# The first load of K in two parts, two small loads moved behind an activation, and w2 in four transfers

## The chip, the cores and the metric

The kernel runs on one core of a Trainium2 chip. The metric is the device time of one execution in microseconds; a time given for a kernel is the median of several executions. A profile comes from one further execution. Its span reaches from the first to the last instruction of the program; the execution's own time is a little longer.

## What is computed

A decoder step for a single token: an adaptive layer norm, attention with 32 query heads over a cache of 8 heads with 32768 positions each, and a small feed-forward layer. Cut to what matters:

```python
mod = (_silu(c) @ w_mod).reshape(c.shape[0], 6, 1, -1)      # c: 512, w_mod: 512 x 3072
sa, ca, ga, sb, cb, gb = (mod[:, i] for i in range(6))
h = _layernorm(x) * (1 + ca) + sa                            # x: one row of 512
q = h @ wq                                                   # 512 x 4096: 32 heads of 128
scores = einsum('bhqd,bhkd->bhqk', q, k) * 128 ** -0.5       # k_cache, v_cache: 8 x 32768 x 128
o = einsum('bhqk,bhkd->bhqd', softmax(scores), v)
x = x + ga * (o @ wo)                                        # wo: 4096 x 512
h = _layernorm(x) * (1 + cb) + sb
x = x + gb * (relu(h @ w1) @ w2)                             # w1: 512 x 1792, w2: 1792 x 512
```

All tensors are bf16. The two caches are 64 MB each, the weights some 15 MB together. All of it is read once, so that the kernel is above all one long stream of loads.

## The kernel before, in words

**The stream of loads.** `load` (L112) issues one load, and `stream_dma` (L154) issues its transfers on SyncE's queue (SP). The list `stream` (L163 to L169) fixes the order once: the first half of K of head 0, w_mod, wq, the second half of K of head 0, then K of the next head and V of this one in turn, for the last heads in halves, and at the end wo in four pieces (`WOP`, L47), w1 in one and w2 in five (`W2P`, L52: pieces of 5, 5, 2, 1 and 1 of the 14 tiles of 512 columns; a tile is 128 KB). `need` (L172) issues the loads of the list up to the one that is asked for.

A whole head of K or V is 8 MB: 128 partitions with 64 KB each, so that partition p holds 256 neighbouring positions of the cache. Half a head is 128 rows of 32 KB. The tiles of the stream come from a pool with three buffers of 64 KB per partition (`ring`, L81). The first of them takes w_mod and wq, the next K of head 0, the third K of head 1; V of head 0 waits until w_mod and wq have been used, and so on around the ring. Each transfer tells of its landing by one of eight semaphores, taken in turn, and a transfer waits until the one eight before it has landed.

The second half of K of head 0 (`UNEVEN`, L57 and L137 to L142) is split: all 128 rows without their last 512 bytes, then these last 512 bytes of 111 rows, then those of the other 17 rows. Behind the issue of V of head 0 stand 14 drains on SP (L145 to L147).

**The start.** `need(("wm",))` (L180) issues the first half of K and w_mod. c and x, one row of 512 each, are loaded by two small transfers on ScalarE's queue (ACT) into eight partitions each (L182 and L183); they are the first thing that ACT does. GpSimd meanwhile makes the identity matrices and constants, `eps_t` among them (L192), and VectorE (DVE) makes masks. When c and x have come, DVE (L248) and four matmuls (L254) turn them into columns (`xc`, L259). From these come silu(c) (`siluT`, L313 to L318, with an exponential on ACT) and the statistics of the layer norm (L282 to L306, with a square root on ACT, for which ACT loads another table of functions). DVE then turns the first half of K (L332). TensorE (PE) multiplies siluT with w_mod (L324) when w_mod has landed, and after the modulation has been brought into columns the first layer norm is applied and multiplied with wq (L396). The query heads are written into a block-diagonal form (`qbd`, L415).

**The heads.** For each head DVE transposes K in place (L441), PE computes the scores (L460), softmax follows (L473 to L509), and PE multiplies with V (L523, for most heads in a hardware loop). PE's and DVE's order is written out by hand (L637 to L735).

**The end.** After V of the last head come the projection with wo (L599 and L605), the second layer norm (L282 to L307), w1 (L765), relu (L776) and w2: for each piece of `W2P`, PE waits for its load and makes four matmuls for each of its tiles (L781 to L791). DVE multiplies by the gate (L793), adds x (L795), and SP stores the row (L796).

Of the kernel before, what the change touches and what calls it, by code (L numbers as in the profile page):

```python
# [9 lines left out]
BF16 = mybir.dt.bfloat16  # L10
F32 = mybir.dt.float32
ACT = mybir.ActivationFunctionType
# [5 lines left out]
def kernel(  # L18
# [14 lines left out]
    nc = tc.nc  # L33
    P = 128
    _, _, D = A_x.shape
# [13 lines left out]
    LAST = Hkv - 1  # L49
    LOOPED = Hkv - 2  # L50
    HALVED = LOOPED - 1
    W2P = [(0, 5), (5, 10), (10, 12), (12, 13), (13, 14)]  # L52
    W1P = [(0, KT)]

    OUT0, OUT1 = 30, 34
# [2 lines left out]
    SPACE = 14  # L58
    assert Dh == 128 and REP == 4 and D == 512 and FT == W2P[-1][1] and NTILE == 4
    scale = float(Dh) ** -0.5  # L60
# [9 lines left out]
    def wo_v(i):  # L70
        g0, n = WOP[i]
        return A_wo[g0 * REP * Dh:(g0 + n) * REP * Dh, :].rearrange("(p r) d -> p r d", p=P)
# [9 lines left out]
    const = ctx.enter_context(tc.tile_pool(name="const", bufs=1))  # L82
# [16 lines left out]
    def room(name, at, shape):  # L99

        n = 2
        for d in shape[1:]:
            n *= d
        return piece(name, at, n)[0:shape[0]].bitcast(F32)

    def piece(name, at, n):

        if name not in pieces:
            pieces[name] = ring.tile([P, NTILE * TK * Dh], BF16, tag="slot", name=name)
        return pieces[name][:, at:at + n]  # L110

    def load(key):  # L112
        kind = key[0]
        if kind == "wm":
            t = piece("wmq_sb", 0, WM).rearrange("p (kt n) -> p kt n", kt=KT)
            src = wm_v
        elif kind == "wq":
            t = piece("wmq_sb", WM, WQ).rearrange("p (kt n) -> p kt n", kt=KT)
            src = wq_v
        elif kind in "kv":  # L120
            g, steps = key[1], key[2]
            src = (kv if kind == "k" else vv)[g, :, TK * steps[0]:TK * (steps[-1] + 1), :]
            name = f"Ksb{g}" if kind == "k" else f"Vsb{g}"
            t = piece(name, TK * Dh * steps[0], TK * Dh * len(steps)).rearrange("p (j d) -> p j d", d=Dh)
        elif kind == "wo":
            g0, n = WOP[key[1]]
            t = piece("tail_sb", g0 * REP * D, n * REP * D).rearrange("p (r d) -> p r d", d=D)
            src = wo_v(key[1])
        elif kind == "w1":
            k0, k1 = W1P[key[1]]  # L130
            t = piece("tail_sb", WO + k0 * Dff, (k1 - k0) * Dff).rearrange("p (kt f) -> p kt f", f=Dff)
            src = w1_v[:, k0:k1]
        else:
            f0, f1 = W2P[key[1]]
            t = piece("tail_sb", WO + KT * Dff + f0 * D, (f1 - f0) * D).rearrange("p (f d) -> p f d", d=D)
            src = w2_v[:, f0:f1]
        if key == UNEVEN:  # L137
            row, src_row = (x.rearrange("p j d -> p (j d)") for x in (t, src))
            for rows, cols in (
                (slice(0, P), slice(0, EDGE)), (slice(0, MOST), slice(EDGE, None)), (slice(MOST, P), slice(EDGE, None)),  # L140
            ):
                stream_dma(row[rows, cols], src_row[rows, cols])  # L142
        else:
            stream_dma(t, src)
        if key[:2] == ("v", 0):  # L145
            for _ in range(SPACE):
                nc.sync.drain()  # L147
        if kind in "kv":
            for i, u in enumerate(steps):
                loaded[(kind, g, u)] = t[:, TK * i:TK * (i + 1), :]  # L150
        else:
            loaded[key] = t

    def stream_dma(dst, src):  # L154
        i = nc.sync.dma_start(out=dst, in_=src)  # L155
        tc.stamp_issue_order_token(i.ins, "sp_stream")
        if last_loop:

            tc.add_manual_dep(i.ins, last_loop[0], mybir.DependencyInfo(
                mybir.DependencyClass.NoSync, mybir.DependencyReason.DATA))  # L160

    whole, halves = [(0, 1, 2, 3)], [(0, 1), (2, 3)]
    stream = [("k", 0, halves[0]), ("wm",), ("wq",), ("k", 0, halves[1])]  # L163
# [4 lines left out]
    stream += [("v", LAST, (0, 1)), ("v", LAST, (2,)), ("v", LAST, (3,))] + [("wo", i) for i in range(len(WOP))]  # L168
    stream += [("w1", i) for i in range(len(W1P))] + [("w2", i) for i in range(len(W2P))]  # L169
    pos = [0]  # L170

    def need(key):  # L172
        while key not in loaded:
            load(stream[pos[0]])
            pos[0] += 1
        return loaded[key]
# [1 line left out]

    piece("wmq_sb", 0, WM + WQ)
    wm_sb = need(("wm",))  # L180
    cx_row = const.tile([16, D // 8], BF16)
    for i, row in enumerate((c[0], A_x[0, 0])):  # L182
        nc.scalar.dma_start(out=cx_row[8 * i:8 * i + 8], in_=row.rearrange("(a n) -> a n", a=8))  # L183

    ident_bf = const.tile([P, P], BF16)
    make_identity(nc, ident_bf[:])
    ident_f = const.tile([P, P], F32)
# [2 lines left out]
    nc.gpsimd.memset(ones_f[:], 1.0)  # L190
    eps_t = const.tile([P, 1], F32)
    nc.gpsimd.memset(eps_t[:], eps)  # L192
    R0 = WM + WQ
    sel = piece("wmq_sb", R0 + 2048, 4 * P).rearrange("p (x c) -> p x c", x=4)
    ib = ident_bf[:]
    nc.vector.tensor_copy(
        out=sel.rearrange("p (h par) (a c) -> p h par a c", h=2, a=4),
        in_=AP(ib.tensor, ib.offset, [ib.ap[0], [64, 2], [1, 2], [0, 4], [2, 32]]),
# [8 lines left out]
        out=mask16.rearrange("p (s q) -> p s q", q=REP),  # L207
        in_=AP(ident_f[:].tensor, ident_f[:].offset, [ident_f[:].ap[0], [0, 4], [1, REP], [REP, P // REP]]),
# [4 lines left out]
    for n in sorted({n * REP for _, n in WOP}):  # L213
        cmask[n] = const.tile([P, P // n], F32, name=f"cmask{n}")
        nc.vector.tensor_reduce(
            out=cmask[n][:], in_=ident_f[:].rearrange("p (c r) -> p c r", r=n), op=ALU.add, axis=AX.X,
# [3 lines left out]
            out=rsel_f[:], in_=ident_f[:].rearrange("p (c r) -> p r c", r=n), op=ALU.add, axis=AX.X,  # L220
# [6 lines left out]
        out=smask[:], in_=ident_f[0:16, 0:16].rearrange("p (s q) -> p s q", q=REP), op=ALU.add, axis=AX.X,  # L227
# [7 lines left out]
        out=place32[:], in_=ident_f[:].rearrange("p (j m) -> p m j", m=32), op=ALU.add, axis=AX.X,  # L235
# [4 lines left out]
        out=rowpick[:, OUT0:OUT1], in_=ident_f[:].rearrange("p (j m) -> p j m", m=32), op=ALU.add, axis=AX.X,  # L240
# [5 lines left out]
    nc.vector.tensor_copy(out=cx_sel[:], in_=cmask[8][0:16, 0:2])  # L246
    cx_bd = piece("wmq_sb", R0 + 2048 + 4 * P, D)[0:16].rearrange("p (b n) -> p b n", b=8)
    nc.vector.tensor_tensor(  # L248
        out=cx_bd, in0=cx_row[:].unsqueeze(1).to_broadcast([16, 8, D // 8]),
# [70 lines left out]
    def to_rows(dst, src_T, w, n):  # L320

        for kt in range(KT):
            for j in range(n):
                nc.tensor.matmul(  # L324
                    dst[j // 4][32 * (j % 4):32 * (j % 4) + 1, :], lhsT=src_T[:, kt:kt + 1],
                    rhs=w[:, kt, j * 512:(j + 1) * 512], start=(kt == 0), stop=(kt == KT - 1),
                    skip_group_check=True,
                )

    for u in range(2):  # L330
        t = need(("k", 0, u)).rearrange("p j d -> p (j d)").bitcast(F32)
# [5 lines left out]
    to_rows(mod_ps, siluT, wm_sb, 6)  # L337
    mod_rows = room("wmq_sb", R0, [P, 2, 512]).rearrange("p (i n) -> p i n", i=2)
    nc.scalar.copy(out=mod_rows[:, 0, :], in_=mod_ps[0])
# [22 lines left out]
    def four_rows(e, name):  # L362

        r_ps = (end_b[0][:, 1, :] if end_b else bank(f"{name}_ps"))[0:OUT1, 0:P]
        nc.tensor.matmul(
            r_ps, lhsT=rowpick[:], rhs=e.rearrange("p m kt -> p (m kt)"), start=True, stop=True,
        )
        return r_ps

    gb_rows = const.tile([OUT1, P], F32)  # L370
    gb_exp = room("wmq_sb", R0 + 2048 + 8 * P, [P, 32, KT]).rearrange("p (m kt) -> p m kt", kt=KT)
    nc.scalar.copy(out=gb_rows[:], in_=four_rows(expand(modT_sb[:, 5 * KT:6 * KT], gb_exp), "gb"))
# [6 lines left out]
        out=nca[:], in0=modT_sb[:, KT:2 * KT], scalar1=-1.0, scalar2=-1.0, op0=ALU.mult, op1=ALU.add,  # L379
# [3 lines left out]
        out=ncb[:], in0=modT_sb[:, 4 * KT:5 * KT], scalar1=-1.0, scalar2=-1.0, op0=ALU.mult, op1=ALU.add,  # L383
# [9 lines left out]
    for kt in range(KT):  # L393
        for i in range(2):
            for a in range(4):
# [3 lines left out]
                )  # L399
    q_cols = room("wmq_sb", R0, [P, 2, 512]).rearrange("p (i n) -> p i n", i=2)  # L400
    qT_sb = const.tile([P, Hq], BF16)
    for i in range(2):
        nc.vector.transpose(out=q_cols[:, i, :], in_=q_ps[i])
        nc.scalar.copy(
            out=qT_sb[:, 16 * i:16 * (i + 1)], in_=q_cols[:, i, :].rearrange("p (h r) -> p h r", r=32)[:, :, 0],
# [231 lines left out]
    with tc.manual_schedule(engines={mybir.EngineType.PE, mybir.EngineType.DVE}):  # L637
# [54 lines left out]
        for u in (2, 3):  # L692
# [49 lines left out]
            out=x1T[:], in0=x1T[:], scalar=1.0, in1=xT, op0=ALU.mult, op1=ALU.add, accum_out=stat2[:, 0:1],  # L742
# [31 lines left out]
        for f0, f1 in ((0, FT // 2), (FT // 2, FT)):  # L774
            nc.vector.transpose(out=hidT[:, f0:f1], in_=hid_v[:, f0:f1])
            nc.scalar.activation(  # L776
                out=AP(hb.tensor, hb.offset + 32 * f0 + 31, [hb.ap[0], [32, f1 - f0]]),
                in_=hidT[:, f0:f1, 0], func=ACT.Relu,
            )

        for part, (f0, f1) in enumerate(W2P):  # L781
            w2_sb = need(("w2", part))
            for ft in range(f0, f1):
                for i in (0, 2, 1, 3):
                    row = OUT0 + i
# [41 lines left out]
```

## Time and profile before

| | |
|---|---|
| time, median of 3 runs | 354.11 us (354.06 to 354.18) |
| profiled execution, its own time | 354.42 us |
| its span | 352.6 us |
| busy: PE, DVE, ACT, POOL | 77%, 55%, 5%, 2% of the span |
| bytes moved by DMA | 149.57 MB, mean 424 GB/s |
| transfers of the stream from issue to landing, median | 33.8 us |

How to read the views: the page gives, for each engine, the share of the span in which it was busy, and for the DMA queues the packets, the megabytes and the time that the packets took as a share of sixteen DMA engines. The view by windows gives the same for stretches of the span: length, busy time of PE, of its weight loads (PEld), DVE, ACT and POOL with the number of instructions in brackets, then the granted clock of PE, the share of the DMA engines and their rate. A packet is counted whole where it starts, so that a short stretch can show a share over 1. The DMA part of a stretch gives the packets, their megabytes and their share for each queue: q1 is SP's queue, q10 is ACT's. The chain of work that ended last is followed back from the last instruction: start, duration, what it was. The timeline has start, duration, engine, line, operation, tiles and, in brackets, how long the engine was idle before and what ended that.

### The profile page before, as it was taken

What the parts mean: (1) busy time and instruction counts of PE and PEld (TensorE: products, weight loads), DVE (VectorE), ACT (ScalarE), POOL (GpSimd) and SP (SyncE); (2) the same over time, 40 slices, a digit from 0 to 9 for tenths busy, and PEclk for the clock granted to TensorE, in tenths of its full rate; (3) what the DMA queues carried; (4) which work ended last, traced back from release to release, by engine and by line L of the source; (5) the groups of instructions that cost most, each with busy time, mean ns of one, the idle gap of its engine ahead of it and who ended that gap; (6) DMA issues with size and microseconds to landing.
All of it is one profiled execution on the core that took longest, in us unless ns stands there. A gap on an engine that the chain in (4) does not pass through costs nothing. (4 is left out here: it accounts for less than half of the span.)

```text
span 352.6 us, 3544 instructions
## 1 busy us (share of the span) xinstructions
PE 272.3 (77%) x1310; PEld 111.8 (32%) x1310; DVE 195.6 (55%) x167; ACT 18.7 (5%) x37; POOL 6.0 (2%) x26
## 2 busy tenths in 40 slices
PE   0054980695999679884988499976999999789994
PEld 0021330232333224331333233322444443234442
DVE  7662563983079513965099316956674293743142
ACT  1200003001000010001000100001000100011000
POOL 3000000000000000000000000000000000000000
PEclk9996895698999969998999979996999999999999
DMA  8999989999999999999999999999999999999995
GB/s 353 404 432 456 468 387 461 446 401 446 439 424 440 416 439 446 401 455 446 409 453 446 409 453 431 426 394 439 446 414 427 450 429 424 431 453 398 432 426 213
DMA packets 5222, 149.57 MB, mean 424 GB/s; under 512 B 604, under 2 KB 988, under 8 KB 1628
## 3 DMA queue, kind: packets, MB, share of 16 engines
q1 hardware_dynamic: 5180, 149.43, 98.5%
q8 instruction: 8, 0.13, 0.1%
q14 instruction: 2, 0.02, 0.0%
q10 hardware_dynamic: 32, 0.00, 0.0%
HBM read 149.42 MB, written 0.00 MB: 424 GB/s over the span
## 5 line engine op out<-in xcount | busy, mean ns | idle before, releaser
L441 DVE STREAM_TRANSPOSE Ksb<-Ksb 128x4096 f32<-128x4096 f32 (+1 forms) x34 | 131.5, 3912 | 57.6 <-DMA Ksb<-in_A_k_cache_dram 57.6
L460 PE MATMUL S_ps<-Ksb,qbd 128*128 128x512 bf16 x512 | 118.9, 385 | 19.2 <-DVE Ksb L441 18.3
L523 PE MATMUL o_ps<-Vsb,P_g 128*16 (+1 forms) x512 | 124.3, 401 | 10.9 <-ACT P_g L497 10.0
L460 PEld LDWEIGHTS <-qbd 128*128 128x128 bf16 x512 | 49.2, 97 | 84.9 <-issue 27.6
L523 PEld LDWEIGHTS o_ps<-Vsb,P_g 128*16 x320 | 30.4, 95 | 60.0 <-issue 31.8
L523 PEld LDWEIGHTS <-P_g 128*16 128x16 bf16 x192 | 16.7, 90 | 22.9 <-issue 0.4
L473 DVE TENSOR_REDUCE m_p<-S_ps 128x1 f32<-128x1024 f32 x7 | 8.6, 1223 | 21.8 <-PE S_ps L460 21.8
L502 DVE STREAM_TRANSPOSE P_g<-P_g 128x1024 bf16<-128x1024 bf16 x8 | 10.0, 1245 | 15.6 <-ACT P_g L497 15.6
L494 ACT ACTIVATE nbias<-Mb_ps 128x1 f32<-128x1 f32 x8 | 1.4, 171 | 269.5 <-PE Mb_ps L492 269.5
L324 PE MATMUL mod_ps<-wmq_sb,siluT 128*1 128x512 bf16 x24 | 3.6, 624 | 9.9 <-DMA wmq_sb<-in_w_mod_dram 9.9
L332 DVE STREAM_TRANSPOSE Ksb<-Ksb 128x4096 f32<-128x4096 f32 x2 | 8.8, 4424 | 1.7 <-DMA Ksb<-in_A_k_cache_dram 1.7
L478 PE MATMUL mT_ps<-ident_f,m_p 128*1 128x128 f32 x8 | 2.2, 270 | 8.9 <-DVE m_p L473 7.9
L497 ACT ACTIVATE P_g<-S_ps,nbias 128x1024 bf16<-128x1024 f32 x8 | 8.9, 1114 | 0.2
L560 PE MATMUL acc_ps<-mask_sb,Y 16*128 16x4 f32 x16 | 3.4, 282 | 5.1 <-DVE Y L556 5.1
L552 DVE SCALAR_TENSOR_TENSOR o_ps<-o_ps,Linv,smask 16x512 f32<-16x512 f32 x8 | 5.8, 720 | 2.8 <-PE o_ps L523 2.8
L254 PE MATMUL xc_ps<-cx_sel,wmq_sb 16*128 16x2 bf16 x4 | 0.3, 172 | 8.7 <-DVE wmq_sb L248 8.7
L590 DVE CAST o_sb<-o_ps 128x4 bf16<-128x4 f32 (+2 forms) x4 | 0.7, 167 | 11.1 <-PE o_ps L586 11.1
L415 POOL TENSOR_TENSOR qbd<-qrep_sb,rowpick 128x64 bf16<-128x64 bf16 x8 | 2.4, 299 | 228.0 <-PE S_ps L460 198.3
L509 DVE RECIPROCAL Linv<-L_ps 16x1 f32<-16x1 f32 x8 | 1.0, 126 | 8.3 <-PE L_ps L506 8.3
L556 DVE TENSOR_REDUCE Y<-o_ps 16x128 f32<-16x512 f32 x8 | 5.4, 679 | 0.3
L635 PE MATMUL spare_ps<-qbd,ident_bf 128*128 128x512 bf16 x18 | 5.4, 381 | 0.0
L396 PE MATMUL q_ps<-wmq_sb,hT 128*1 128x512 bf16 x32 | 3.6, 626 | 2.3 <-DMA wmq_sb<-in_A_wq_dram 2.3
(114 smaller groups left out, 71.6 us busy)
## 6 DMA issues: line engine op xcount, KB each, us to landing
Ksb<-in_A_k_cache_dram SPq DMA_DIRECT2D x5, 4096.0 KB, 22.9
Vsb<-in_A_v_cache_dram SPq DMA_DIRECT2D x5, 4096.0 KB, 36.5
wmq_sb<-in_A_wq_dram SPq DMA_DIRECT2D x1, 4096.0 KB, 28.1
Vsb<-in_A_v_cache_dram SPq DMA_DIRECT2D x2, 2048.0 KB, 41.1
Ksb<-in_A_k_cache_dram SPq DMA_DIRECT2D x1, 4032.0 KB, 37.2
wmq_sb<-in_w_mod_dram SPq DMA_DIRECT2D x1, 3072.0 KB, 18.9
tail_sb<-in_A_wo_dram SPq DMA_DIRECT2D x1, 2048.0 KB, 23.2
tail_sb<-in_B_w_dram SPq DMA_DIRECT2D x1, 1792.0 KB, 30.6
```

What stands on the lines that cost most here:

```text
L324: nc.tensor.matmul(dst[j // 4][32 * (j % 4):32 * (j % 4) + 1, :], lhsT=src_T[:, kt:kt + 1], rhs=w[:, kt, j * 512:(j + 1) * 512], start=(kt ...
L332: nc.vector.transpose(out=t, in_=t)
L396: nc.tensor.matmul(q_ps[i][32 * a:32 * a + 1, :].rearrange("o (h e) -> o h e", e=32), lhsT=hT[:, kt:kt + 1], rhs=wq_f[:, kt, i, a], start= ...
L441: t = nc.vector.transpose(out=KTt.bitcast(F32), in_=KTt.bitcast(F32))
L460: nc.tensor.matmul(S_ps_tiles[g], lhsT=qbd[g % 2][:, hp, 4 * (7 - s):4 * (7 - s) + P], rhs=KTv[:, 16 * sl:16 * sl + 16, h, :, par], start= ...
L473: behind_loop(nc.vector.reduce_max(out=m_p[:], in_=S_g.rearrange("p g f -> p (g f)"), axis=AX.X))
L497: nc.scalar.activation(out=P_g[:], in_=S_g.rearrange("p g f -> p (g f)"), func=ACT.Exp, bias=nbias[:], scale=scale, accum_out=l_g[:],)
L502: behind_loop(nc.vector.transpose(out=P_g[:], in_=P_g[:]))
L523: nc.tensor.matmul(o_tiles[g][:], lhsT=PT, rhs=Vx, start=first, stop=False, skip_group_check=True)
L552: nc.vector.scalar_tensor_tensor(out=o, in0=o, scalar=Linv_tiles.pop(g)[:], in1=smask[:].unsqueeze(2).to_broadcast([16, 4, Dh]), op0=ALU.m ...
L556: nc.vector.tensor_reduce(out=Y[:], in_=o.rearrange("p s d -> p d s"), op=ALU.add, axis=AX.X)
L635: nc.tensor.matmul(spare[0], lhsT=ident_bf[:], rhs=qbd[0][:, :, 0:P], start=True, stop=True)
```

## The change

Three edits. The first transfer of the stream, the first half of K of head 0, is issued as 16 rows and then the other 112. The transfers of c and x are written behind `eps_t`, and behind a new activation on one element of it; a dependency without a semaphore keeps them behind that activation in ACT's own order. And w2 comes in pieces of 6, 5, 2 and 1 tiles.

```diff
-    W2P = [(0, 5), (5, 10), (10, 12), (12, 13), (13, 14)]
+    W2P = [(0, 6), (6, 11), (11, 13), (13, 14)]
...
                 stream_dma(row[rows, cols], src_row[rows, cols])
+        elif key == stream[0]:
+            for rows in (slice(0, 16), slice(16, P)):
+                stream_dma(t[rows], src[rows])
         else:
             stream_dma(t, src)
...
     wm_sb = need(("wm",))
-    cx_row = const.tile([16, D // 8], BF16)
-    for i, row in enumerate((c[0], A_x[0, 0])):
-        nc.scalar.dma_start(out=cx_row[8 * i:8 * i + 8], in_=row.rearrange("(a n) -> a n", a=8))
-
     ident_bf = const.tile([P, P], BF16)
...
     nc.gpsimd.memset(eps_t[:], eps)
+    warm = const.tile([1, 1], F32)
+    first = nc.scalar.activation(out=warm[:], in_=eps_t[0:1], func=ACT.Exp)
+    cx_row = const.tile([16, D // 8], BF16)
+    for i, row in enumerate((c[0], A_x[0, 0])):
+        d = nc.scalar.dma_start(out=cx_row[8 * i:8 * i + 8], in_=row.rearrange("(a n) -> a n", a=8))
+        tc.add_manual_dep(d.ins, first.ins.name, mybir.DependencyInfo(
+            mybir.DependencyClass.NoSync, mybir.DependencyReason.DATA))
```

In the built program SP has as many transfers as before, one more at the front and one fewer at the end. ACT's first table load now stands ahead of c and x, with the new activation. The semaphores of the transfers move by one: the 17-row piece of K's second half now waits for the sixteen rows of the first half, K of head 1 for c. On DVE the reciprocal of the first layer norm (L306) stands ahead of the transposes of K (L332) instead of behind them.

## The prediction

> **What bounds the kernel now.** I read the page first (busy shares, DMA queues), then the chain of work that ended last in order of time, then stretches of DMA traffic.
>
> ```profile
> DMA  8999989999999999999999999999999999999995
> q1 hardware_dynamic: 5180, 149.43, 98.5%
> 338.50 11.12 DMA tail_sb<-in_B_w_dram
> 349.62 0.04 issue
> 349.66 0.29 PE end_ps L788 x4
> 349.95 0.02 issue
> 349.98 0.29 DVE o_rows L793
> 350.27 0.02 issue
> 350.30 0.28 DVE o_bf L795
> ```
>
> One queue, the one that SP issues to, carries 149.43 MB and keeps the sixteen DMA engines busy for 98.5% of the span. The two slices below 9 tenths that matter are the first and the last. The chain ends with the last weight transfer, landing at 349.62, and 1 us of small work behind it. Three stretches of 4.83 us, from the view by windows, show that nothing is lost in between:
>
> ```profile
> 43.43:48.26 4.83, 4.83 (x24) 2.12 (x23) 4.75 (x3) 0.00 (x0) 0.00 (x0) 1.00 1.01 436
> 60.00:64.83 4.83, 0.06 (x1) 0.16 (x2) 4.55 (x2) 0.00 (x0) 0.00 (x0) 0.50 1.00 434
> 79.00:83.83 4.83, 2.88 (x13) 1.07 (x11) 1.72 (x3) 0.00 (x0) 0.30 (x1) 1.00 1.00 434
> ```
>
> The last two columns are the DMA share (1.00) and the rate (434 GB/s), whatever PE and DVE do. So the time is: when the engines get their first bytes, plus what each has to move, plus the tail. Every engine works through its own list in order; a microsecond lost by one engine at the start is still missing at the end. That decides how the change is to be priced: only its first and last transfers, and anything that makes an engine stand still.
>
> **The rate of one engine, and the start.** The DMA part for a stretch in the middle (63.00 to 67.83 us), then the first transfers by windows of 0.2 us, then the DMA part for 1.7 to 2.7 us:
>
> ```profile
> q1 hardware_dynamic: 32, 2.10, 100.2%
> ```
> ```profile
> 1.50:1.70 0.20, 0.00 (x0) 0.00 (x0) 0.20 (x1) 0.03 (x1) 0.20 (x2) 1.00 0.02 3
> 1.70:1.90 0.20, 0.00 (x0) 0.00 (x0) 0.20 (x2) 0.20 (x1) 0.20 (x3) 1.00 2.95 821
> 1.90:2.10 0.20, 0.00 (x0) 0.00 (x0) 0.20 (x2) 0.20 (x1) 0.20 (x1) 1.00 3.54 984
> 2.10:2.30 0.20, 0.00 (x0) 0.00 (x0) 0.20 (x1) 0.20 (x1) 0.20 (x1) 1.00 1.42 492
> 2.30:2.50 0.20, 0.00 (x0) 0.00 (x0) 0.20 (x1) 0.20 (x1) 0.20 (x2) 1.00 0.45 164
> 2.50:2.70 0.20, 0.00 (x0) 0.00 (x0) 0.20 (x1) 0.20 (x1) 0.20 (x1) 1.00 0.44 164
> ```
> ```profile
> q1 hardware_dynamic: 16, 0.52, 175.6%
> ```
>
> In the middle, 32 packets of 64 KB take 1.002 x 16 x 4.828 / 32 = 2.42 us each: 27.1 GB/s for one engine, so a row of 32 KB takes 1.21 us. A packet is counted where it starts, and 164 GB/s in 0.2 us is one packet of 32 KB: 5, 6, 3, 1 and 1 engines begin in the five windows, on average at 2.04 us, the last one 0.8 us behind the first. These sixteen first packets take 1.756 x 16 x 1.0 / 16 = 1.76 us each, 0.55 us more than later ones.
>
> **Part 1, c and x behind an activation.** The timeline around them:
>
> ```profile
> 0.73 0.59 ACTq L183 DMA_DIRECT2D cx_row<-in_c_dram  x1
> 0.74 0.38 SPq L155 DMA_DIRECT2D Ksb<-in_A_k_cache_dram  x1
> 1.35 0.28 ACTq L183 DMA_DIRECT2D cx_row<-in_A_x_dram  x1
> 1.67 1.28 ACT L313 ACT_TABLE_LOAD   x1 [1.67 <-PEq L811]
> 1.73 0.10 POOL L192 MEMSET eps_t<- 128x1 f32 x1
> 2.12 20.71 SPq L155 DMA_DIRECT2D Ksb<-in_A_k_cache_dram  x4
> 7.99 0.68 DVE L248 TENSOR_TENSOR wmq_sb<-cx_row,pick 16x512 bf16<-16x512 bf16 x1 [1.50 <-DMA cx_row<-in_A_x_dram]
> 10.98 0.16 DVE L318 TENSOR_TENSOR siluT<-xc,sig 128x4 bf16<-128x4 f32 x1
> 12.85 8.77 DVE L332 STREAM_TRANSPOSE Ksb<-Ksb 128x4096 f32<-128x4096 f32 x2 [1.71 <-DMA Ksb<-in_A_k_cache_dram]
> 20.11 3.57 PE L324 MATMUL mod_ps<-wmq_sb,siluT 128*1 128x512 bf16 x24 [9.91 <-DMA wmq_sb<-in_w_mod_dram]
> ```
>
> The table load moves up to about 0.73 and ends near 2.0; eps_t is there at 1.83; the activation takes some 0.2 us; c is issued near 2.2 for 0.73, x near 2.8. They then queue behind more rows of K on each engine: x took 6.6 us from issue to the multiplication at 7.99, so it would come near 9.5, and up to 8 us later if those rows are slow. siluT (11.14) has 9 us until w_mod lands at 20.1, and w_mod moves with the same queue. Cost: nothing; uncovered it would be 1.5 us. What ACT does behind it (L313 on) waits for xc anyhow. The gain: c is generated at the same moment as K's first descriptors, and its issue takes 0.59 us where x takes 0.28. Up to 0.3 us earlier start for K, counted below.
>
> The extra transfer at the front shifts the eight DMA semaphores: the 17-row piece of K's second half now waits until the sixteen rows have landed, K of head 1 for c. Queued behind both on SP is the whole stream. But SP's first four K issues already end only at 22.83 (2.12 + 20.71), and the engines come to what is behind them after 38 us. Covered by 15 us.
>
> **Part 2, sixteen rows, then 112.** For it: every engine gets one descriptor at once. If all begin with the first window, 2.04 - 1.8 = 0.24 us, with c out of the way up to 0.3 more. I take 0.4.
>
> Against it: those sixteen rows go to sixteen neighbouring partitions, and the sixteen engines write there together. In a 128-row load each engine has eight partitions. The trace has one place where engines write into the partitions of others: the odd pieces of K's second half (111 and 17 rows of 512 B) near 39 us, while the other thirteen engines are already on K of head 1. The DMA parts for 38.60 to 38.98, 38.98 to 39.40 and 41.20 to 42.00 us:
>
> ```profile
> DMA packets 64, 0.87 MB, mean 2291 GB/s; under 512 B 15, under 2 KB 51, under 8 KB 51
> ## 3 DMA queue, kind: packets, MB, share of 16 engines
> q1 hardware_dynamic: 64, 0.87, 576.3%
> ```
> ```profile
> q1 hardware_dynamic: 54, 0.03, 21.7%
> ```
> ```profile
> q1 hardware_dynamic: 12, 0.79, 232.6%
> ```
>
> The middle one is short rows alone: 0.217 x 16 x 0.42 / 54 = 27 ns each. In the first, 13 packets are over 8 KB; 5.763 x 16 x 0.38 = 35.04 us, less 36 x 0.027 and about 0.14 for 15 completions, leaves 33.93, or 2.61 us each. The third has their second packets: 2.326 x 16 x 0.8 / 12 = 2.48. Against 2.42 each of the thirteen loses 0.19 + 0.06 = 0.25 us, and the 128 short rows are eight for each engine's eight partitions: 32 ns a row, where its bytes alone are 19 ns. I read this as a path into a group of partitions that has one engine's rate and is shared. It is an inference: a slower memory would look alike.
>
> If so, the sixteen rows take 16 x 1.21 / G us, with G such groups among sixteen partitions. Ends: G = 16, no sharing, 1.21; G = 2 (eight neighbours a group), 9.7. The trace does not show which eight partitions are a group. I take the middle step, G = 4: **4.84 us, 3.63 more** than now.
>
> [...]
>
> The 112 rows are seven for each engine, and runs of seven no longer lie on the groups of eight. Ends: none meets another, nothing; each meets another all the time, 7 x 1.21 = 8.5 us. I let the worst engine meet one other in three of its seven rows: **3.6 us**. The worst engine counts, since the end waits for the last.
>
> **Part 3, w2 in four.** The last piece (one tile, 128 KB) stays. Each engine has eight packets and one completion fewer; at the tail (DMA part for 349.0 to 349.3 us)
>
> ```profile
> q1 hardware_dynamic: 23, 0.02, 16.6%
> ```
>
> a packet takes 0.166 x 16 x 0.3 / 23 = 35 ns, most of it bytes. Ends: 0 and 9 x 0.02 = 0.2; I take 0.05 us gained. The piece before the last now feeds eight matmuls; four take 0.29 us at the end (chain), so at worst they push the last four back by 0.3, at best not at all. I take 0.
>
> **Sum.** 354.42 us is the profiled execution (span 352.6, 1.8 around it), 0.31 over the median of the three runs, 354.11. 354.42 + 3.63 + 3.64 - 0.4 - 0.05 = 361.2; against the median **360.9 us**.
>
> **Rivals.**
> - *No shared path* (other side). The thirteen engines lost their 0.25 us to something else, and sixteen engines may write to sixteen partitions at full rate. Then only the start counts: 0.1 us (stagger gone, first packets longer) to 0.9 (0.24 + 0.3 + part of the 0.55 + w2). I take 0.5: 353.6. It decides if all the sharing costs less than 0.5 us. For it: the 512 B rows themselves never took over 27 ns beside busy engines. Against it: the loss where they crossed. 0.30.
> - *The rows stay with their engines.* The sixteen rows are dealt to the engines that have these partitions in a 128-row load, so nothing crosses, but few engines start early, and the change does not do what it says: 354.0. 0.05.
> - *Row by row.* Of the 112 rows each engine takes every sixteenth, and all move together over sixteen neighbours: 8 x 4.84 = 38.7 us for 9.7, 29 more: 383. 0.04.
> - The forecast: 0.61, by itself from 357.5 (second term nothing) to 363 (both terms some way up).
>
> **Numbers.** About 0.2% (0.7 us) is what a measurement here tells from no change. Faster by more: 0.08, the better quarter of the first rival. Within: 0.22 of it and 0.05 of the second, 0.27. Slower: 0.61 + 0.04 = 0.65. Cases of both signs hold much of the chance, so the range goes from the first rival's middle to the top of the forecast: 353.5 to 363, which leaves out about 0.2.
>
> **What would show it.** The first transposes of K (at 12.85) would begin near 19.5 to 20, and the rate from 2 to 6 us would be near 110 GB/s instead of some 400. Under the first rival they begin near 12.4 and the sixteen first packets start within one window. w_mod's first matmul (20.11) shifts by what the worst engine lost, and so must the last transfer's landing (349.62); if the start is late by 7 us and the end is not, the engines were not bound by their lists. If siluT is what PE's first modulation matmul waits for, part 1 was not covered. If the last four matmuls begin later than 0.1 us after the landing, part 3 costs.

## The result, and the profile after

The changed kernel takes 363.8 us beside 354.14 us for the kernel before on the same chip: **2.73% slower**, ratio 1.0273 (95% interval 1.0258 to 1.0288). The 363.8 is the median of four executions (363.5 to 364.2); two more of the same kernel fell in a slower state (371 and 374 us) and are left out, as such ones are in every time below. The profiled execution took 363.5 us with a span of 361.2, so 2.3 around it; before it was 354.42, 352.6 and 1.8. The direction and the mechanism were forecast; the size was not: 360.9 was predicted, with 363.0 as the upper end.

From the page of after, the span, the rate in 40 slices of 9 us, and the queue that carries the stream:

```profile
span 361.2 us, 3546 instructions
GB/s 174 247 343 448 440 432 465 421 399 457 457 428 399 452 450 428 414 452 435 421 435 443 435 428 435 445 399 425 432 432 434 435 432 434 432 435 414 428 425 222
q1 hardware_dynamic: 5052, 149.43, 98.5%
```

The same rates from the page of before:

```profile
GB/s 353 404 432 456 468 387 461 446 401 446 439 424 440 416 439 446 401 455 446 409 453 446 409 453 431 426 394 439 446 414 427 450 429 424 431 453 398 432 426 213
```

The bytes are the same, and the queue is as busy as before (98.5%). Nearly the whole loss lies in the first three slices. Note that the busy share does not show it: an engine that is held up in the middle of a packet counts as busy (98.5% with first packets of 3.77 us as with 1.76). From the fourth slice on the rates are those of before.

The start by windows (the last two columns are the share of the DMA engines and the rate):

```profile
1.70:3.00 1.30, 0.00 (x0) 0.00 (x0) 1.30 (x2) 0.51 (x2) 1.30 (x5) 1.00 2.90 403
2.00:6.00 4.00, 0.00 (x0) 0.00 (x0) 4.00 (x10) 0.21 (x2) 1.66 (x7) 1.00 0.67 107
4.80:19.30 14.50, 0.33 (x5) 0.28 (x5) 2.94 (x16) 0.41 (x2) 0.57 (x3) 1.00 1.03 253
20.00:21.50 1.50, 0.00 (x0) 0.08 (x1) 0.50 (x5) 0.67 (x2) 0.00 (x0) 1.00 0.97 262
```

In the first window lie the sixteen first packets, one for each engine: 2.90 x 1.30 = 3.77 us each, where before they took 1.76. The third window holds the 112 rows, seven for each engine: 1.03 x 14.5 / 7 = 2.1 us a row instead of 1.21. The fourth has the first packet of w_mod on each engine: 0.97 x 1.5 = 1.45 us where its 24 KB need 0.91. Together 2.0 + 6.3 + 0.5 = 8.8 us. (6.3 is 14.8 us for the seven rows, by the packets themselves, less 7 x 1.21.) From 2 to 6 us the rate is 107 GB/s, where the forecast said 110. That this fits so well is luck: a window counts a packet where it starts, and here it holds 4 of the sixteen rows and 9 of the slow rows behind them. In `x16_near` below, where the same sixteen rows are followed by ordinary ones, the same window has 147:

```profile
2.00:6.00 4.00, 0.00 (x0) 0.00 (x0) 3.31 (x13) 0.96 (x1) 1.71 (x7) 1.00 0.86 147
```

From the first start (1.78) to the last end (6.28) the sixteen rows move at some 117 GB/s.

The timeline of after, rows around the first edit and the first work on K:

```profile
0.73 1.28 ACT L193 ACT_TABLE_LOAD   x1 [0.73 <-PEq L817]
1.86 0.58 ACTq L196 DMA_DIRECT2D cx_row<-in_c_dram  x1
2.48 0.28 ACTq L196 DMA_DIRECT2D cx_row<-in_A_x_dram  x1
17.61 0.68 DVE L254 TENSOR_TENSOR wmq_sb<-cx_row,pick 16x512 bf16<-16x512 bf16 x1 [11.12 <-DMA cx_row<-in_A_x_dram]
20.18 0.15 DVE L324 TENSOR_TENSOR siluT<-xc,sig 128x4 bf16<-128x4 f32 x1
22.60 8.77 DVE L338 STREAM_TRANSPOSE Ksb<-Ksb 128x4096 f32<-128x4096 f32 x2 [1.73 <-DMA Ksb<-in_A_k_cache_dram]
29.78 1.45 PE L330 MATMUL mod_ps<-wmq_sb,siluT 128*1 128x512 bf16 x12 [9.97 <-DMA wmq_sb<-in_w_mod_dram]
```

K of head 0 is turned from 22.60 instead of 12.85, and w_mod is multiplied from 29.78 instead of 20.11: 9.7 us later. (The forecast had K at 19.5 to 20.) c and x come 9.6 us later too (17.61 for 7.99), but siluT is there at 20.33, 9 us before w_mod, whose landing is what PE waits for (9.97 us, ended by the DMA). The last rows of the chain of waits:

```profile
334.98 22.23 DMA tail_sb<-in_B_w_dram
357.21 0.04 issue
357.25 1.27 PE end_ps L794 x32
358.52 0.02 issue
358.54 0.29 DVE o_rows L799
```

(The wait that ends at 357.21 is for an earlier piece of w2 than in the chain of before; the 32 matmuls behind it use the last pieces too. By its packets the stream ends at 357.90 instead of 349.29.) The multiplication by the gate begins at 358.54 instead of 349.98: **8.56 us later**. Nearly all that was lost at the start is still missing 340 us later, as forecast for engines that work through lists. Behind it 2.66 us are left to the end of the span, before 2.62. The other 0.5 us lies around the span (2.3 for 1.8). 8.56 + 0.04 + 0.5 = 9.1, which is 363.5 less 354.42.

### The profile page after: what moved, and what is told of

Same layout as the page of the kernel before. It is cut to its first block, busy times and chain, and to the rows that moved or that the text cites. A ratio compares the mean times of both kernels' runs of the same rounds, so it can differ in the third digit from the quotient of the medians.

```text
span 361.2 us, 3546 instructions
## 1 busy us (share of the span) xinstructions
PE 273.6 (76%) x1310; PEld 111.9 (31%) x1310; DVE 195.5 (54%) x167; ACT 18.9 (5%) x38; POOL 6.0 (2%) x26
## 3 DMA queue, kind: packets, MB, share of 16 engines
q1 hardware_dynamic: 5052, 149.43, 98.5%
```

## The experiments

**The three edits one by one.** `only_rows` is the kernel before with the split of the first load alone; `no_rows` has the other two edits without it; `by_cols` is the changed kernel, with the first load split along the row instead:

```diff
-            for rows in (slice(0, 16), slice(16, P)):
-                stream_dma(t[rows], src[rows])
+            for js in (slice(0, 16), slice(16, 2 * TK)):
+                stream_dma(t[:, js], src[:, js])
```

> The kernel before with part 2 alone (16 rows, then 112). Shared path into groups of partitions: the whole loss comes back, 363 to 365 us, the first transposes of K begin near 22.6 us. Rival, c and x or w2 at fault: within 0.5 us of 354.1.

Measured: 364.78 us beside 354.24, ratio 1.03 (1.0284 to 1.0317). K is turned from 22.69. The split alone makes the whole loss, and some 1.0 us more than the three edits together; 0.7 of that lies behind the store (see the closing waits below).

> The changed kernel without part 2: c and x behind the activation, w2 in four, the first load whole. Shared path: nothing crosses, 353.8 to 354.3 us. Rival, c and x or w2 at fault: 362 to 365.

Measured: 354.59 us beside 354.24, ratio 1.0012 (1.0002 to 1.0021). Part 1 and part 3 cost almost nothing, and gain nothing.

> The changed kernel with the first load split by columns: 16 of the 128 positions of every partition first (4 KB a row, 128 rows), then the other 112. As many transfers and the same shift of the semaphores as in the changed kernel, but every engine keeps its partitions. Shared path: 353.6 to 354.4 us, K lands near 12.8. Rival, the additional transfer at the front or its semaphore: 363 to 365.

Measured: 354.99 us, ratio 1.0017 (1.0008 to 1.0027). K is turned from 13.39, 0.5 us later than before. With a further transfer at the front, all 128 partitions wide, the three edits cost some 0.6 us, 1.0 at most. So it is the rows, not the second transfer.

> The kernel before with c and x behind the activation alone; as many transfers as before. By the prediction covered: 353.8 to 354.3 us. The start of the sixteen engines is no earlier (c was not in the way), so no gain over 0.1 us.

Measured, with c and x behind the activation alone: 354.17 us beside 354.14, ratio 1.0002 (0.9992 to 1.0012). No difference, so no earlier start either.

> The kernel before with w2 in four transfers alone. By the prediction 0.05 us less. By the profile of the two parts together, where the last store's semaphore was waited for later in the closing list than before and the engines were done earlier: 354.4 to 354.7, the loss behind the store (from the store's issue to the end 2.5 us for 2.0), not before it.

Measured, with w2 in four pieces alone (the line `W2P` of the change): 354.71 us beside 354.14, ratio 1.0014 (1.0004 to 1.0024): slightly slower, not faster. In the profile the store is issued at 350.56 as before (350.61), so the loss lies behind it.

**What the sixteen rows cost, and where the paths lie.** `halves64` splits the first load at row 64 instead of row 16. It and the kernels that follow ran once each; what they show rests on their traces, and on differences of a microsecond and more.

> The changed kernel with the first load as 64 and 64 rows. Every engine has four neighbouring partitions, so that runs are regular. Shared path, groups of which two engines' runs fall into one: every packet takes twice 1.21 us, K's first half lands 9 to 10 us later than before, 363 to 365 us. Rival, the memory side (the first sixteen rows lie in one megabyte, which sixteen engines read at once): the rows of 64 are spread over four, so less than half of the loss, under 359 us.

Measured: 365.23 us; K is turned from 23.50. The view by windows of halves64, a stretch that holds one row of each engine (262 GB/s in 2 us are sixteen rows of 32 KB):

```profile
6.40:8.40 2.00, 0.00 (x0) 0.00 (x0) 0.08 (x1) 0.00 (x0) 0.00 (x0) 1.00 1.28 262
```

1.28 x 2.00 = 2.56 us a row, slightly more than twice 1.21, as if with 64 neighbouring rows two engines shared each path. The next three put sixteen more rows of 32 KB in front of everything in the kernel before, into a tile that is loaded again later (so the output's computation is unchanged); only the partitions differ:

```diff
+    piece("Ksb0", 0, 1)
+    x1 = piece("Ksb1", 0, 2 * TK * Dh).rearrange("p (j d) -> p j d", d=Dh)
+    stream_dma(x1[0:16], kv[1][0:16, 0:2 * TK, :])      # x16_near; x16_by4: 0:64:4; x16_by8: 0:128:8
     wm_sb = need(("wm",))
```

> The kernel before with one transfer more, ahead of all: 16 rows of 32 KB of head 1's K, into partitions 0 to 15 of head 1's buffer (written again with the whole head later). Their bytes alone are 1.2 us for each engine. Shared path, four groups among sixteen neighbours: 4.4 to 5 us over before, the first sixteen packets some 4 us each. Groups of eight neighbours: near 9. Rival, no sharing on the way into the partitions: 1.2 over before.

> The same sixteen rows of memory, into partitions 0, 4, 8 and so on to 60. Shared path with groups of four neighbours, two of which share: two engines a path, 2.4 us over before, packets of 2.4 us. Memory side at fault: as with neighbouring partitions, since the source is the same.

> The same sixteen rows of memory, into partitions 0, 8, 16 and so on to 120. Groups of eight neighbours: no two engines meet, 1.2 us over before. [...] Memory side: as the other two.

Measured, beside 354.12: 359.25, 357.35 and 357.54 us. The stretch of the sixteen first packets by windows, in x16_near, in x16_by4 and in x16_by8:

```profile
1.70:3.00 1.30, 0.00 (x0) 0.00 (x0) 1.30 (x4) 1.26 (x1) 1.30 (x5) 1.00 2.89 404
```
```profile
2.10:3.20 1.10, 0.00 (x0) 0.00 (x0) 1.10 (x3) 0.84 (x1) 0.97 (x3) 1.00 1.94 477
```
```profile
2.10:3.20 1.10, 0.00 (x0) 0.00 (x0) 1.10 (x3) 0.85 (x1) 0.97 (x3) 1.00 2.03 477
```

3.76, 2.13 and 2.23 us for a first packet (1.76 in the kernel before). Beyond their bytes (1.21) and the 0.7 us that any extra load costs at the end (see the closing waits), the sixteen rows cost 3.2, 1.3 and 1.5 us; in the last two some 0.5 us of this is a later start of the first packets (2.52 and 2.53 us on average, 2.06 in x16_near). Sixteen neighbours cost most, a stride of 4 or 8 about the same. The source rows are the same three times, so a slower memory does not explain the difference. That a stride of 8 is no better than one of 4 speaks against paths of eight neighbours. One map of the paths fits all three, and the runs below test it: four neighbours and the four that lie 32 higher are one path, so that sixteen neighbours reach four paths (3.76 us) and both strides reach eight (2.13 and 2.23).

**What the 112 rows cost.** Here the same place in the code loads 112 rows, to partitions 16 to 127 (`x112`) or 0 to 111 (`x112_low`); or 96 rows, to partitions 32 to 127 (`x96`); or, as a control, 128 rows (`x128`).

> The kernel before with 112 rows of 32 KB of head 1's K ahead of all, into partitions 16 to 127: the second part of the split alone. Bytes alone: 7 x 1.21 = 8.5 us. By the prediction's term (three of seven rows meet one other) 12 over before; by what the changed kernel's start shows, 14 to 15; no sharing, 8.5.

> The kernel before, with 128 more rows of 32 KB (to all 128 partitions) loaded in front of everything; they land in a tile that is loaded again later. The control for the 112 extra rows. If it is the meeting of engines on one path that costs, 128 rows, dealt as the ordinary load deals them, cost their bytes alone: packets of about 1.21 us from the second on, K's first row ends at 3.77 + 8 x 1.21 = 13.5 us, and the time is 354.1 + 9.7 + 0.7 (end of the program) = 364.5. If a further large transfer ahead of K costs something by itself, or the start of the stream is slow for the first ten microseconds whatever is loaded, packets stay near 2 us, K's first row ends near 18 to 19, and the time is 369 to 371.

> The kernel before, with 112 more rows of 32 KB in front of everything, as with the 112 extra rows before, but to partitions 0 to 111 instead of 16 to 127. If each engine takes seven neighbouring rows and the meeting of engines on one path of four neighbours (with the four that lie 32 higher) holds all of them up, nothing changes much: 5 to 6 us beyond the bytes of 8.49, K's first row ends near 17.5 to 18.3, time 369 to 370. If the extra cost came from where the block lies (partitions 16 to 127, behind a free block), the loss beyond the bytes goes and the time is near 363.5.

> The kernel before, with 96 more rows of 32 KB to partitions 32 to 127 in front of everything: six rows for each engine, bytes 7.28 us. By a model in which paths of four partitions (shared with the four 32 higher) are independent of each other, the sixteen engines lose 2.2 us on average beyond the bytes, the worst 5.4, and they end K's first row far apart (spread of some 5 us). If meeting on one path holds up the others too, all engines end K's first row within 1 us of each other, 4 to 5.5 us beyond the bytes: 15 to 16.5 us; time 354.1 + 7.3 + 4 to 5.5 + 0.7 = 366.1 to 367.6.

Measured: x112 369.38 us beside 354.12; x128 364.69, x112_low 369.08 and x96 369.02 beside 354.41. Fewer rows take longer. By windows, seven packets of each engine in x128 and in x112, and one of each in two stretches of x96:

```profile
3.30:11.30 8.00, 0.85 (x6) 0.79 (x7) 3.90 (x20) 0.77 (x2) 0.64 (x4) 1.00 1.07 459
```
```profile
3.90:16.90 13.00, 0.85 (x6) 0.79 (x7) 3.47 (x19) 1.78 (x3) 0.39 (x2) 1.00 1.06 282
```
```profile
8.50:10.50 2.00, 0.00 (x0) 0.00 (x0) 0.00 (x0) 0.00 (x0) 0.00 (x0) 1.00 1.28 263
11.00:13.00 2.00, 0.00 (x0) 0.00 (x0) 0.40 (x1) 0.00 (x0) 0.00 (x0) 1.00 1.13 262
```

1.07 x 8.0 / 7 = 1.22 us a row in the control, 1.06 x 13.0 / 7 = 1.97 in x112, 1.28 x 2.0 = 2.56 and 1.13 x 2.0 = 2.26 in x96, where the other stretches lie between these two. The transposes of K on the timelines of x128, x112 and x96 give the loss (12.85 before):

```profile
22.45 8.77 DVE L335 STREAM_TRANSPOSE Ksb<-Ksb 128x4096 f32<-128x4096 f32 x2 [9.93 <-DMA Ksb<-in_A_k_cache_dram]
```
```profile
27.43 8.77 DVE L335 STREAM_TRANSPOSE Ksb<-Ksb 128x4096 f32<-128x4096 f32 x2 [11.47 <-DMA Ksb<-in_A_k_cache_dram]
```
```profile
27.09 4.45 DVE L335 STREAM_TRANSPOSE Ksb<-Ksb 128x4096 f32<-128x4096 f32 x1 [9.96 <-DMA Ksb<-in_A_k_cache_dram]
```

9.60, 14.58 and 14.24 us later, of which 8, 7 and 6 rows at 1.21 are bytes: 9.70, 8.49 and 7.28. So 128 rows cost their bytes alone, 112 rows 6.1 us more and 96 rows 7.0 more. A model with paths that don't hinder each other gave x96 a mean loss of 2.2 and a spread of 5 us; all sixteen engines ended K's first row within half a microsecond of each other. The other theory, that a meeting holds up all, gave 4 to 5.5 us; its one pace came out, its size was too small. The place of the block (x112_low) hardly matters.

**Does one shared path hold up the others?** First three rows only, to partitions 64 to 66 (`x3_far`, by the map three engines into the path of a fourth) or to 0, 4 and 8 (`x3_own`, by the map no meeting).

> The kernel before with three rows of 32 KB ahead of all (head 1's K, into its own buffer), by three engines into partitions 64 to 66, all in the four of one other engine. How far does sharing reach? If it stays on that path: three engines and that one stand for some 4.9 us, the other twelve run at 1.21 us a row from the start, 300 GB/s and more from 4 to 7 us; 358 to 359 us, since the end waits for the last. If engines hold each other up beyond the path: every engine's rows are slow until the three have landed, under 200 GB/s.

> The control: the same three rows into partitions 0, 4 and 8, where these engines write in any 128-row load. Shared path: no sharing, three engines are 1.21 us later, 354.5 to 355.5 us. Rival, an additional small transfer in front is what costs: as x3_far.

Measured: 357.4 and 356.1 us, beside 354.14. (x3_own is 2.0 us later, a row and the 0.7 us of the closing waits, which its expectation left out.) The stretch from 4 to 7 us by windows, x3_far, then x3_own:

```profile
4.00:7.00 3.00, 0.00 (x0) 0.00 (x0) 1.30 (x7) 0.00 (x0) 0.36 (x2) 1.00 0.91 306
```
```profile
4.00:7.00 3.00, 0.41 (x5) 0.36 (x5) 2.32 (x12) 0.20 (x1) 0.36 (x2) 1.00 1.05 437
```

306 GB/s just meets the first theory (300 and more) and is far from the second (under 200), while the time is below the first theory's 358 to 359. But the first theory also wanted twelve engines at 1.21 us from the start, and that is not so: in x3_far the first packet of every engine took 1.97 us or more (2.89 on average), those of the twelve engines that by the map have a path to themselves among them, while x3_own has 1.60 on average, and 1.29 and 1.24 in the rows behind; in x3_far too the rows behind are soon at 1.21 again. (That every engine has a path of its own in a 128-row load is read from the 1.22 us a row of x128; that the three rows of x3_own went to the paths of their own engines, from their meeting nobody.) So neither theory holds as it stands.

Then the same 64 rows of 32 KB at three places: partitions 32 to 95, 36 to 99 and 0 to 63.

> The kernel before, with 64 more rows of 32 KB to partitions 32 to 95 in front of everything, four neighbouring rows for each engine. If a path is four neighbouring partitions with the four that lie 32 higher, these sixteen blocks of four lie on sixteen different paths, although they are only half the partitions: no engine meets another, the rows cost their bytes alone (4 x 1.21 = 4.85), packets are near 1.21 us from the second on, and the time is 354.2 + 4.85 + 0.7 = 359.7. If fewer partitions are slower in themselves, or any block that is not all 128 rows costs, the rows take as long as those of partitions 0 to 63: some 2.5 us each, 10 in all, and the time is 365. [...]

> The same 64 rows to partitions 36 to 99. By the same map fourteen engines have a path to themselves and two, the first and the last, share one for all four rows. If paths are independent, the fourteen keep 1.21 us a row and the two take 2.42: the sixteen ends of K's first row lie some 5 us apart, and since the end waits for the last engine, the time is 354.2 + 4.85 + 4.85 + 0.7 = 364.6. If one shared path holds up all engines, all sixteen go at one pace between 1.21 and 2.42 (1.6 to 1.95 as in the ranks of the 112 rows where by the map two engines meet), their ends lie within 1 us of each other, and the time is 354.2 + 4 x 1.75 + 0.7 = 362, from 361.3 to 362.7.

> The same 64 rows to partitions 0 to 63. By the map all sixteen engines share paths two by two: 2.5 us a row, four rows 10.2 with 4.85 of bytes, and the time is 354.2 + 10.2 + 0.7 = 365.1. If the number of partitions doesn't matter and something else does, it is as fast as partitions 32 to 95: near 359.7.

Measured: 360.03, 365.75 and 365.44 us, beside 354.14. One row of each engine by windows in x64_mid, then in x64_low:

```profile
5.20:6.20 1.00, 0.00 (x0) 0.00 (x0) 0.22 (x2) 0.00 (x0) 0.00 (x0) 1.00 1.22 524
```
```profile
6.75:8.75 2.00, 0.00 (x0) 0.00 (x0) 0.00 (x0) 0.00 (x0) 0.00 (x0) 1.00 1.29 263
```

1.22 us against 2.58, with the same rows from the same memory and the same number of partitions. Together with the three sets of sixteen rows this bears the map out: sixteen blocks of four on sixteen paths cost nothing, on eight paths twice the time. The forecast was made from the map, and the time agrees with it to 0.3 us (360.03 for 359.7; the first packets begin 0.3 us later than before, at 2.34 on average). No packet's record names its partition or its engine, so that the map stands on these times alone.

x64_one came out as neither theory said. (By the map the rows that meet are those to partitions 64 to 67 and 96 to 99, the eighth and the last block of four, and not the first and the last, as its expectation has it.) Two stretches by windows, the first with one row of every engine, the second with sixteen packets:

```profile
3.90:4.90 1.00, 0.00 (x0) 0.00 (x0) 1.00 (x7) 0.00 (x0) 0.39 (x2) 1.00 1.39 525
10.76:12.41 1.65, 0.00 (x0) 0.08 (x1) 0.66 (x5) 1.28 (x1) 0.00 (x0) 1.00 0.91 318
```

In the first, 1.39 us on average is fourteen packets of 1.23 and two of 2.42: the two that meet share, and the others do not notice. In the second all sixteen packets take 0.91 x 1.65 = 1.50 us; they belong to thirteen engines. The other three are then in packets of 4.0 us, begun earlier. By the map, the two late engines write their last extra rows where a third already has its rows of K, and the thirteen others, each on a path of its own, go at 1.50 until about 15 us. So two on a path left the others alone (1.23 us), three on a path went with a quarter more time for the other thirteen (1.50). The independent model (364.6) was nearer, and still 1.15 us short.

**The closing waits.** After the store SP waits for the semaphores of the transfers, before the program ends. The store in the timelines of only_w2, no_rows and only_rows, whose spans end at 353.1, 352.6 and 362.2:

```profile
350.56 0.29 SPq L796 DMA_DIRECT2D out_dram<-o_bf  x1
```
```profile
350.11 0.29 SPq L799 DMA_DIRECT2D out_dram<-o_bf  x1
```
```profile
359.50 0.29 SPq L799 DMA_DIRECT2D out_dram<-o_bf  x1
```

From issue to the end of the span that is 2.5, 2.5 and 2.7 us; before (350.61) and after (359.17) it is 2.0. SP's waits in the tail, only_w2 and then only_rows:

```profile
SPq L822 <- DMA out_dram<-o_bf: 0.6, 1, 0.6
```
```profile
SPq L825 <- DMA out_dram<-o_bf: 0.8, 1, 0.8
```

Before and after have no such row. The three kernels with the wait have a number of transfers on SP other than before, and so have the kernels with an extra load, which all show it too; by_cols, only_cx and halves64, with as many transfers as before, do not, and end 2.0 us after the store's issue. I read this so: with another number of transfers the store gets another of the eight semaphores, one that SP waits for earlier in its closing list; what stands behind it then runs after the landing and not beside it. The change has one transfer more and one fewer, the store keeps its semaphore, and the end keeps its 2.0 us. The link to the number of transfers is shown by these traces; the order of the list is inferred, and no kernel was made to test it alone. The kernels with an extra load pay the same 0.7 us (hence the 0.7 in the later expectations).

## Why the prediction was wrong in its size

- *The stream bounds the kernel, and a loss at the start stays.* Right: 9.7 us at K, 8.56 us at the gate. The loss did not shrink by more than about 0.3 us between the first w_mod packet and the end.
- *The reading of 0.25 us as a shared path.* Right in what it led to. It was an inference from short rows in the middle of the stream; x64_mid and x64_low show shared paths directly, though no run shows that the 0.25 us came from them. The groups aren't eight neighbours, as the prediction has it: the runs fit four neighbours with the four that lie 32 higher (2.13 us in x16_by4 and 2.23 in x16_by8, 1.22 in x64_mid and 2.58 in x64_low). For sixteen neighbours that gives the middle step G = 4, for which the prediction had no row of the trace.
- *Sixteen rows, 3.63 us.* About right. The first packets lost 2.0 us themselves, and some of what the next ones lost is theirs as well: in x16_near, where 128 ordinary rows follow, the whole cost beyond the bytes was 359.25 - 354.12 - 1.21 - 0.7 = 3.2, so that the term was 0.4 too large.
- *"I let the worst engine meet one other in three of its seven rows: 3.6 us."* **This step failed.** The 112 rows cost 6.1 us beyond their bytes by themselves (x112), 6.3 in the changed kernel. The term counted one engine's meetings, as if the engines on paths of their own went on at 1.21 us; in the runs no engine was the worst one, and all sixteen moved at 2.1 us a row. The bounds 0 to 8.5 held, but the range's upper end (both terms "some way up") reached only 2.1 us over the forecast, and 2.9 were needed.
- *Start, 0.4 us gained.* Wrong, nothing. The sixteen first packets still begin between 1.78 and 2.55 us, on average at 2.01 (before 2.04), so it isn't the number of rows per engine that staggers them; only_cx shows that c was not in the way.
- *Part 1 covered, semaphores covered.* Right: siluT 9 us before w_mod. c and x came 9.6 us later, at 17.61, which is what the prediction allowed (9.5 and up to 8 more).
- *Part 3, 0.05 us gained.* Right as far as the store. From the end of the stream's last packet to the issue of the store it is 1.26 us, before 1.31. What the term left out is the semaphore of the store: alone the edit costs 0.14%, some 0.5 us.
- *Around the span.* Not in the sum: 0.5 us. The other kernels that split the first load show it too (only_rows 2.4, halves64 2.4, by_cols 2.2), those with an extra load don't (x128 1.8). The cause is open.

With the measured terms the sum is 354.42 + 2.0 + 6.3 + 0.5 - 0.2 + 0.5 = 363.5, where -0.2 is what came back on the way.

**Still open.** Why 112 and 96 rows go at one pace on all engines. (A rank is here the n-th row of every engine.) If each engine takes seven neighbouring rows, the map says that only two or four engines meet at a time; in x112 the ranks with two (1.95 and 1.62 us a row) are indeed faster than those with four (2.0 to 2.2), but in x96 the ranks with four and with six do not differ so (2.56, and 2.26 to 2.54). And x64_one shows two engines meeting without the others noticing (1.23 us), so a meeting of pairs alone does not explain it; in x64_one's later part (1.50 us for thirteen engines) and in x3_far (2.89 us for the first packets) the rest went slower while, by the map, three or four were on one path. Which of these rows each engine gets is not in the trace. Nor is the reading side excluded for these loads: x112 and x112_low read the same rows of memory, and no run reads them in runs of seven to partitions that keep apart. No run here shows by which way the holding-up spreads.

## What to carry to other kernels

Price a load by the partitions that its rows go to, and not by its bytes alone: here 64 rows cost 5.2 us at partitions 32 to 95 and 10.6 at 0 to 63, and 112 rows took longer than 128 (369.38 us for 364.69). If the first load has to be cut, cut it along the row and keep all partitions (some 0.6 us here, for 10 by rows). In this kernel, whose transfers work through lists without a gap, what was lost in the first 20 us was paid nearly in full at the end (8.56 us of 9.7), though the busy share of the queue stayed the same (98.5%).

## What was not expected of the hardware

- Where all sixteen engines met in pairs, a row took 2.56 us, where two rows' bytes are 2.42 (the one pair of x64_one kept 2.42); three that were on one path by the map took 4.0 where 3.63 are bytes, and meanwhile thirteen others went from 1.21 to 1.50 us.
- Two engines on one path left the fourteen others at 1.21 to 1.23 us (x64_one).
- The number of transfers on SP's queue decided over 0.5 to 0.7 us behind the last store; that it does so by the store's semaphore is inferred.
- The first packets of the stream began over 0.8 us, whether each engine had one row waiting (1.78 to 2.55 us) or eight (1.76 to 2.60).
